# Attention, two products and a routed expert layer on one core: conversion, weight product and the next stage's first products moved to later slots

## The chip, the core and the metric

The kernel runs on one core of a Trainium2 chip. Five engines each run their own instruction stream in order: TensorE (PE, with its weight loads shown apart as PEld), VectorE (DVE), ScalarE (ACT), GpSimd (POOL) and SyncE (SP), which here issues almost all DMAs. The metric is the time of one execution in microseconds; lower is better.

## The reference, cut to what matters

```python
# attention, B=2, H=8, S=768, D=64: a query sees only keys of its own hash bucket (6 sign bits)
mask = q_bucket[:, :, :, None] == k_bucket[:, :, None, :]
scores = np.where(mask, scale * q @ k.T, -1e9)
attn = softmax(scores); x = (attn @ v) laid out as [1536, 512]
# second part
h = (x @ w1) * (x @ w2) @ w3           # d_ff = 1024
x = h @ w_out                          # [1536, 512]
# third part: each token goes to the one expert of 8 with the largest logit
logits = x @ w_gate + modality_bias[modality_id]
out[mask] = gate_w[mask] * (relu(x[mask] @ e_w1[e]) @ e_w2[e])
```

All of it is float32. A product is made of three products of rounded high and low parts (`TERMS`). `w3 @ w_out` is formed once in the kernel (the "weight product", called w34), so that the second part is `(a * b) @ w34`.

## The kernel before

The heads are taken in pairs: 8 pairs of 2 heads, 6 query tiles each. Everything up to the middle of the kernel is one loop over slots `i` from 0 to 109. A slot's work is written out by hand, and each engine keeps the written order:

- **First products and maxima** (`stage_1`, unit `i`, slots 0 to 95): PE forms a tile of scores `m` (2 matmuls), and DVE takes its row maximum (`TENSOR_REDUCE`, line 348). After 6 units (3 query tiles of 2 heads) four small operations (lines 352 to 355, result `nm`) prepare the maxima; they run on POOL. `stage_f` transposes them on PE (`f`), ACT copies them (`rT`), and two DMAs put them as two extra rows under `q`.
- **Second products** (`stage_2`, unit `j = i - 9`, slots 9 to 104): PE forms the scores `s` with the maximum already subtracted (4 matmuls), ACT takes the exponential into `pt` (line 377), and POOL adds `pt` into `acc`. `stage_a` multiplies `pt` with `v` two slots later (`a`, 4 matmuls). In slots 25 to 84 (`GROUP`) two of these are done together in every second slot. `z`, `n`, `wt`, `pg` are small products for hash bits, row sums and the gate's weights.
- **Conversion**: `w1`, `w2`, `w3`, `w_out` arrive as 64-bit numbers and are made float32 on DVE in 3 steps for each of 40 pieces (`L508`, `L509`, `L498`, issued by `fill`). A piece of `w3` or `w_out` is split into its high part on ACT and its low part on POOL (line 490); a piece of `w1` or `w2` goes out to DRAM (`wfd`). `RAMP` says how many pieces are wanted by which slot, and `piece_load` brings a piece in.
- **Weight product** (`w34_step`): 192 matmuls `w` in 8 rounds of 24, at `W34_STEP` for each slot and at most 7 at once, as soon as their pieces are converted. After a round ACT copies PSUM out (`ev`), and only then the next round can begin.
- **SWITCH** (slot 86): the 40 pieces and 192 matmuls are done, their memory is given back, and the 16 pieces of `w1` and `w2` come back from DRAM (`st`), are split on ACT and DVE (line 490), `RATE2` of them for each slot. From `SWITCH + NSTEP` the first chunk of tokens is split as well (`norm_step`).
- **The next stage's first products** (`moe_half`, `ab`, 12 matmuls): from slot `EARLY` = 95 one half for each slot, until `NEARLY` = 5 of the first chunk's 8 columns are done. The rest follows behind the loop, without the attention's work beside it.

Scores `m` and `s` share one PSUM tag with two buffers; which of the two a tile gets is settled when the program is built. So an `m` waits either for the reduction of the `m` before it (DVE), or, where the two have changed places, for the exponential of the `s` just ahead of it (ACT).

At the start PE fills gaps with products of the unit matrix (`busy`). SP's queue is in written order too: `load_pair` brings `q` and `k` of a pair (384 KB each), a piece is 512 KB.

The lines around the first slots:

```python
        if i == 4:
            load_pair(2)
        if i == 5:
            for m in range(3):
                piece_load(m)
        if i == 8:
            load_pair(3)
```

Of the kernel before, what the change touches and what calls it, by code (L numbers as in the profile page):

```python
# [8 lines left out]
F32 = mybir.dt.float32  # L9
# [4 lines left out]
ALU = mybir.AluOpType  # L14
# [11 lines left out]
C_MASK = float(2 ** 30)  # L26
# [6 lines left out]
NCH = NT // CH  # L33

PRE = 0
RAMP = ((7, 0), (19, 10), (84, 41))
RATE2 = 1.4
W34_STEP = 3.15
W34_MOST = 7
SWITCH = 86  # L40
LEAD = 9
NDVE = 0
ACC_DVE = ((76, ()), (96, (2,)))
# [2 lines left out]
RUN = 2  # L46
NP = 4
BUSY = {4: 2, 5: 4, 8: 2}
GROUP = (16, 76)
HASH = (4, 6)  # L50
PREL = 2
PREA = 2
# [2 lines left out]
HS = S // 2  # L55
KROWS = (78, 128)
NB = 12
EARLY = 95
ERATE = 1
NEARLY = 5  # L60
NSTEP = 4
PATTERN = (1, 1, 0, 1, 0)
HOOKS = (3, 24, 82)
RAWS = 4
# [34 lines left out]
def pieces_at(i):  # L99
    for (a, x), (b, y) in zip(RAMP, RAMP[1:]):  # L100
        if i < b:
# [62 lines left out]
def body(tc, qT, kT, vP, w1d, w2d, w3d, wod, mod, wgate, mbias, e1, e2, cst, out):  # L164
    nc = tc.nc
    PE, ACT, DVE, POOL, SP = nc.tensor, nc.scalar, nc.vector, nc.gpsimd, nc.sync
# [61 lines left out]
    NU = 2 * 6 * NPAIR  # L228
    raw_t, bt_t, head_t, v_t = {}, {}, {}, {}

    def load_pair(p):
        b, hp = divmod(p, HP)
        for nm, src in (("q", qT), ("k", kT)):
            t = r_raw([P, S])
            SP.dma_start(t, src[b, hp])
            raw_t[p, nm] = t
# [99 lines left out]
    def stage_1(u):  # L336
        p, qt, hd = u
        q, k = head_t[p, hd, "q"], head_t[p, hd, "k"]
        s = ps("s", [P, 2, 512], f"m{p}_{qt}_{hd}")
        for half in range(2):  # L340
            PE.matmul(  # L341
                s[:, half, 0:HS], q[0:KROWS[hd], 0, qt * P:qt * P + P], k[0:KROWS[hd], 0, half * HS:half * HS + HS],
                start=True, stop=True,
            )
        if qt % 3 == 0 and hd == 0:
            nm_t[p, qt // 3] = r_nm([P, 32])
        nm = nm_t[p, qt // 3]
        DVE.tensor_reduce(nm[:, 3 * hd + qt % 3:3 * hd + qt % 3 + 1], s[:, :, 0:HS], AX.XY, ALU.max, negate=True)  # L348
        if qt % 3 == 2 and hd == 1:
            v, fin = nm[:, 6:12], nm[:, 12:24].bitcast(F32R).rearrange("p (d x t) -> p d x t", d=2, x=2)  # L350
            v3 = v.rearrange("p (d t) -> p d t", d=2)
            POOL.tensor_scalar(v, nm[:, 0:6], C_MASK / 2, None, ALU.is_lt)
            POOL.tensor_mul(v, v, nm[:, 0:6])
            POOL.tensor_copy(fin[:, :, 0, :], v3)
            POOL.tensor_sub(fin[:, :, 1, :], v3, fin[:, :, 0, :].bitcast(F32))

    def stage_f(p, half):
        t = ps("m", [P, P], f"f{p}_{half}")
        PE.transpose(t[0:12, :], nm_t.pop((p, half))[:, 12:24], ident)
        rT = r_rT([12, P], F32R)  # L360
        ACT.copy(rT, t[0:12, :])  # L361
        for hd in range(2):
            r = brow(hd) + NB
            SP.dma_start(
                head_t[p, hd, "q"][r:r + 2, 0, half * HS:half * HS + HS].bitcast(F32),
                rT[6 * hd:6 * hd + 6, :].bitcast(F32),
            )
# [301 lines left out]
    def moe_half(ch, f, j, tag="ab"):  # L669
        x = x_t[ch]  # L670
        fs = slice(f * P, f * P + P)
        if j == 0:
            ab_t[ch, f] = ps(tag, [P, 2, CH], f"ab{ch}{f}")
        ab = ab_t[ch, f]
        for c in range(4):
            for i, (st, mv) in enumerate(TERMS):
                PE.matmul(ab[:, j, :], w12[j][:, st, c, fs], x[:, mv, c, :], start=(c == 0 and i == 0), stop=(c == 3 and i == 2))  # L677
        if j == 0:
            return
        if f % 4 == 0:  # L680
            gf_t[ch, f // 4] = rg["gf"]([P, 4, CH])
        gf = gf_t[ch, f // 4][:, f % 4, :]
        g = g_t[ch]
        asb = rg["asb"]([P, CH])
        ACT.copy(asb, ab[:, 0, :])  # L685
        DVE.tensor_mul(gf, asb, ab[:, 1, :])  # L686
        ACT.copy(g[:, 0, f, :], gf)  # L687
        POOL.tensor_sub(g[:, 1, f, :], gf, g[:, 0, f, :].bitcast(F32))  # L688
# [39 lines left out]
    for c in (102, 128):  # L728
        v = cs[:, c:c + 28].rearrange("p (j n) -> p j n", n=NB + 2)[:, :, 0:6]
# [47 lines left out]
    for i in range(NU + LEAD + NLAG + 1):  # L777
# [14 lines left out]
            rg["asb"] = ring("asb", CH, 1, True)  # L792
        if i == 0:
            load_v(0)
        if i == 4:
            load_pair(2)
        if i == 5:
            for m in range(3):
                piece_load(m)
        if i == 8:  # L800
            load_pair(3)
        if i == 12:
            SP.dma_start(cs[:, 160:], cst[:, 160:])
            SP.dma_start(wgs[:, :, 0:E], wgate.rearrange("(c p) e -> p c e", p=P))
        if 0 <= i - SWITCH - NSTEP < HP + 2:
# [18 lines left out]
        p, ph = divmod(i, 12)  # L824
# [3 lines left out]
        if i < NU:  # L828
            if p and ph == 9 and p + 3 < NPAIR:
                load_pair(p + 3)  # L830
            stage_1(units[i])
            fill()
            if long:
                fill()
        fi = i if i <= 6 else i - 1
        if fi % 6 == 0 and 0 < fi <= NU and (i <= 6 or fi > 6):
            stage_f(*divmod(fi // 6 - 1, 2))
        if p == 0 and ph in (1, 2):
            hash_z([1], ph - 1, "uw"[ph - 1])
# [34 lines left out]
            w34_step(quota - done["w"])  # L874
        for h in range(int((i - EARLY) * ERATE), int((i - EARLY + 1) * ERATE)):
            if 0 <= h < 2 * NEARLY:
                moe_half(0, h // 2, h % 2, "wm"[h // 2 % 2])
        if late and n % 12 == 4:
            late.pop(0)()
        if not both or len(dq) > 2:  # L880
# [298 lines left out]
    wu = {}  # L1179
# [360 lines left out]
```

## Time and profile before

| | |
|---|---|
| median of 3 runs | 686.21 us (685.7 to 687.42) |
| the profiled execution: its own time | 685.69 us |
| the profiled execution: span, first to last instruction | 683.9 us |
| PE busy | 651.8 us of the span (95%) |
| DVE, POOL, ACT busy | 386.3, 317.8, 314.0 us |
| granted clock of PE, mean | 0.998 of 2.4 GHz |

The span is 1.8 us shorter than the execution's own time. A row of the stretches gives start and end, length, each engine's busy time with its instructions in the order PE, PEld, DVE, ACT, POOL, then PE's granted clock (1.00 is 2.4 GHz), the DMA engines' busy share and GB/s. A row of the timeline gives an instruction's start, how long it took, the engine and line, what it writes and reads, how many were merged, and in brackets how long the engine sat idle just before and what released it. A matmul's time includes its way through the pipeline, so rows of PE overlap: what a group costs PE is read from one group's start to the next.

### The profile page before, as it was taken

The numbers are of one execution on the slowest core, as the hardware profiler recorded it, in microseconds if no ns is written. First come the engines' busy times: TensorE is split into PE (matmuls) and PEld (weight loads), VectorE is DVE, ScalarE is ACT, GpSimd is POOL, SyncE is SP. The second block draws the span as 40 slices with busy tenths as digits, with TensorE's granted clock in tenths as the row PEclk, the third lists the DMA queues.
The fourth block names the chain that finished last, engine by engine and source line by source line (L and its number), as shares of the span: only waits on it lengthen the run. The fifth ranks groups of instructions, "written<-read, shape, count | busy, mean of one in ns | idle before, by whom it ended". The sixth has DMA issues, their size and how long they took to land. (4 is left out here: it accounts for less than half of the span.)

```text
span 683.9 us, 11034 instructions
## 1 busy us (share of the span) xinstructions
PE 651.8 (95%) x4038; PEld 511.9 (75%) x4038; DVE 386.3 (56%) x617; ACT 314.0 (46%) x534; POOL 317.8 (46%) x312
## 2 busy tenths in 40 slices
PE   7888999999999997999999999999999999999995
PEld 2544566666566754678989898989888899899984
DVE  6897676767586889642632121121275865575550
ACT  7264665556556556553422121221224665564551
POOL 7498888687858776552524233231214212111110
PEclk9999999999999999999999999999999999999999
DMA  8755555473736463303201010100036977766630
GB/s 225 239 187 171 186 150 199 120 234 112 223 111 205 137 203 108 105 20 96 65 16 47 16 47 16 47 1 32 1 121 221 333 267 238 238 205 212 209 115 19
DMA packets 41691, 94.04 MB, mean 138 GB/s; under 512 B 6352, under 2 KB 12032, under 8 KB 41632
## 3 DMA queue, kind: packets, MB, share of 16 engines
q1 hardware_dynamic: 39552, 86.72, 40.7%
q0 software_dynamic: 2080, 6.56, 2.8%
q8 instruction: 34, 0.56, 0.4%
q14 instruction: 25, 0.20, 0.1%
HBM read 72.98 MB, written 12.94 MB: 126 GB/s over the span
## 5 line engine op out<-in xcount | busy, mean ns | idle before, releaser
L677 PE MATMUL ab<-x,w 128*128 128x256 f32 x1152 | 143.6, 284 | 1.3 <-ACT rT L361 0.7
L677 PEld LDWEIGHTS ab<-x,w 128*128 128x128 f32 x1152 | 140.6, 191 | 5.6 <-ACT asb L685 2.1
L383 POOL TENSOR_TENSOR acc<-acc,pt 128x770 f32<-128x770 f32 x61 | 113.5, 1861 | 23.8 <-ACT pt L377 21.3
L348 DVE TENSOR_REDUCE nm<-m 128x1 f32<-128x768 f32 x96 | 91.4, 955 | 56.7 <-PE m L341 56.5
L377 ACT ACTIVATE pt<-s 128x768 f32<-128x768 f32 x96 | 78.0, 813 | 89.3 <-PE s L376 86.2
L376 PEld LDWEIGHTS s<-q,k 128*128 128x128 f32 (+1 forms) x384 | 63.9, 189 | 43.8 <-issue 23.2
L376 PE MATMUL s<-q,k 128*128 128x384 f32 (+1 forms) x384 | 91.5, 360 | 2.8 <-ACT pt L377 2.1
L688 POOL TENSOR_TENSOR g<-gf,g 128x256 fp32r<-128x256 f32 x48 | 35.6, 741 | 123.1 <-ACT g L687 119.8
L1206 DVE TENSOR_TENSOR eu<-er,eu 128x1024 fp32r<-128x1024 f32 x56 | 68.0, 1232 | 23.4 <-ACT eu L1205 21.6
L391 PE MATMUL a<-pt,v 128*64 128x385 f32 x384 | 76.4, 504 | 0.0
L686 DVE TENSOR_TENSOR gf<-asb,ab 128x256 f32<-128x256 f32 x48 | 20.2, 421 | 97.0 <-ACT asb L685 96.9
L1369 PE MATMUL e1F<-ex,eu 128*128 128x256 f32 x576 | 70.3, 283 | 0.5 <-DVE ex L1335 0.3
L1369 PEld LDWEIGHTS e1F<-ex,eu 128*128 128x128 f32 x576 | 69.7, 190 | 1.4 <-DVE ex L1335 0.5
L1395 POOL DMA_INDIRECT out<-o,sidx x13 | 13.7, 1051 | 122.3 <-ACT o L1394 106.2
L1387 PE MATMUL e2F<-eu,h 128*128 128x512 f32 x288 | 68.8, 394 | 0.0
L341 PE MATMUL m<-k,q 78*128 78x384 f32 x192 | 52.0, 353 | 11.1 <-ACT pt L377 5.7
L1387 PEld LDWEIGHTS e2F<-eu,h 128*128 128x128 f32 x288 | 53.3, 188 | 11.1
L1205 ACT CAST eu<-er 128x1024 fp32r<-128x1024 f32 x56 | 57.6, 1046 | 8.1 <-DMA er<-e 7.8
L1002 PE MATMUL x2p<-w,g 128*128 128x512 f32 x240 | 58.1, 396 | 0.0
L591 PE MATMUL w<-wo,w 128*128 128x512 f32 x192 | 51.4, 400 | 2.2 <-ACT ev L594 1.6
L1002 PEld LDWEIGHTS x2p<-w,g 128*128 128x128 f32 x240 | 44.2, 188 | 11.4 <-issue 2.1
L685 ACT COPY asb<-ab 128x256 f32<-128x256 f32 x48 | 17.9, 373 | 73.7 <-PE ab L677 73.7
(203 smaller groups left out, 800.1 us busy)
## 6 DMA issues: line engine op xcount, KB each, us to landing
er<-e SPq DMA_DIRECT2D x56, 512.0 KB
cr<-w3d SPq DMA_DIRECT2D x16, 512.0 KB
cr<-wod SPq DMA_DIRECT2D x8, 512.0 KB
cr<-w1d SPq DMA_DIRECT2D x8, 512.0 KB
wfd<-cT SPq DMA_DIRECT2D x16, 256.0 KB
cr<-w2d SPq DMA_DIRECT2D x8, 512.0 KB
st<-wfd SPq DMA_DIRECT2D x16, 256.0 KB
raw<-kT SPq DMA_DIRECT2D x8, 384.0 KB
```

The source lines that it names most:

```text
L341: PE.matmul(s[:, half, 0:HS], q[0:KROWS[hd], 0, qt * P:qt * P + P], k[0:KROWS[hd], 0, half * HS:half * HS + HS], start=True, stop=True,)
L348: DVE.tensor_reduce(nm[:, 3 * hd + qt % 3:3 * hd + qt % 3 + 1], s[:, :, 0:HS], AX.XY, ALU.max, negate=True)
L376: PE.matmul(s[:, hd, 0:HS], k[0:n, i, c * P:c * P + P], q[0:n, i, cl], start=(i == 0), stop=(i == 1))
L377: ACT.activation(pts[j % NP][:, :, 0:HS], s[:, :, 0:HS], AF.Exp, scale=SCALE)
L383: (DVE if on_dve else POOL).tensor_add(acc, pts[(j - 1) % NP] if c == 1 else acc, pts[j % NP])
L391: PE.matmul(a_t[p, half][64 * hd:64 * hd + 64, :], v[:, c, 64 * hd:64 * hd + 64], pts[j % NP][:, hd, :], start=(c == 0), stop=(c == QT - 1 ...
L677: PE.matmul(ab[:, j, :], w12[j][:, st, c, fs], x[:, mv, c, :], start=(c == 0 and i == 0), stop=(c == 3 and i == 2))
L1002: PE.matmul(st["ps"], g_t[ch][:, a, f, i * P:i * P + P], w34[b][:, f, :], start=(f == 0 and k == 0), stop=(f == 7 and k == 2),)
L1205: ACT.copy(t[:, 0, sl], raw)
L1206: DVE.tensor_sub(t[:, 1, sl], raw, t[:, 0, sl].bitcast(F32))
L1369: PE.matmul(o[f], w[:, st, c, fs], x[:, mv, c, :], start=(c == 0 and i == 0), stop=(c == 3 and i == 2))
L1387: PE.matmul(o, h[:, st, f, sl], w[:, mv, f, :], start=(f == 0 and k == 0), stop=(f == 7 and k == 2))
```

## The change

Numbers that set the order are replaced, the four small operations on the first pair's maxima go from POOL to DVE, the first pair's first `stage_f` is written ahead of unit 6 and not behind it, and the loads of the third and fourth pair, of the first three pieces and of two small tables are written 1 to 3 slots later. `moe_half` takes its PSUM under tags `w` and `u` in turn (it was `w` and `m`).

```diff
-RAMP = ((7, 0), (19, 10), (84, 41))
-RATE2 = 1.4
-W34_STEP = 3.15
+RAMP = ((8, 0), (22, 8), (89, 41))
+RATE2 = 1.6
+W34_STEP = 3.25
-SWITCH = 86
+SWITCH = 92
-GROUP = (16, 76)
+GROUP = (18, 82)
-EARLY = 95
+EARLY = 101
-NEARLY = 5
-NSTEP = 4
+NEARLY = 4
+NSTEP = 2
...
-            POOL.tensor_scalar(v, nm[:, 0:6], C_MASK / 2, None, ALU.is_lt)
-            POOL.tensor_mul(v, v, nm[:, 0:6])
...
+            eng = DVE if p == 0 else POOL
+            eng.tensor_scalar(v, nm[:, 0:6], C_MASK / 2, None, ALU.is_lt)
+            eng.tensor_mul(v, v, nm[:, 0:6])
...
-        if i == 4:
+        if i == 7:
             load_pair(2)
-        if i == 5:
+        if i == 8:
             for m in range(3):
                 piece_load(m)
-        if i == 8:
+        if i == 11:
             load_pair(3)
-        if i == 12:
+        if i == 13:
...
+            if i == 6:
+                stage_f(0, 0)
             stage_1(units[i])
...
-        fi = i if i <= 6 else i - 1
-        if fi % 6 == 0 and 0 < fi <= NU and (i <= 6 or fi > 6):
+        fi = i - 1
+        if fi % 6 == 0 and 6 < fi <= NU:
             stage_f(*divmod(fi // 6 - 1, 2))
...
-                moe_half(0, h // 2, h % 2, "wm"[h // 2 % 2])
+                moe_half(0, h // 2, h % 2, "wu"[h // 2 % 2])
```

**DVE, slots 9 to 13.** Before, three conversion steps stand behind the reductions of slots 10 and 11, and so on in every slot to 14 (`u`, `cT` are a piece's steps; `m_5_0` is pair 0's tile 5, head 0):

```order
L348 TENSOR_REDUCE nm_226<-m_4_1_259 128x1
L348 TENSOR_REDUCE nm_226<-m_5_0_274 128x1
L508 TENSOR_SCALAR u_279<-cr_202 128x512
L509 SCALAR_TENSOR_TENSOR u_279<-cr_202,u_279 128x512
L498 SCALAR_TENSOR_TENSOR cT_278<-cr_202,u_294 128x512
L348 TENSOR_REDUCE nm_226<-m_5_1_295 128x1
```

Of the change, the same engine at the same place:

```order
L348 TENSOR_REDUCE nm_222<-m_4_1_255 128x1
L348 TENSOR_REDUCE nm_222<-m_5_0_270 128x1
L348 TENSOR_REDUCE nm_222<-m_5_1_286 128x1
L353 TENSOR_SCALAR nm_222<-nm_222 128x6
L354 TENSOR_TENSOR nm_222<-nm_222 128x6
L355 CAST nm_222<-nm_222 128x2x3
L356 TENSOR_TENSOR nm_222<-nm_222 128x2x3
L509 TENSOR_SCALAR u_295<-cr_235 128x512
L510 SCALAR_TENSOR_TENSOR u_295<-cr_235,u_295 128x512
L499 SCALAR_TENSOR_TENSOR cT_294<-cr_235,u_295 128x512
L348 TENSOR_REDUCE nm_316<-m_0_0_313 128x1
L348 TENSOR_REDUCE nm_316<-m_0_1_331 128x1
```

The first piece stands in slot 11, behind the four small operations, and slots 12 and 14 have no piece; up to slot 23 eight pieces are done in slots 11, 13, 15, 16, 18, 20, 22 and 23.

**SP, around the first maxima's transfers (`rT`).** Before:

```order
L235 DMA raw_187<-qT 128x768
L235 DMA raw_189<-kT 128x768
L305 DMA k_18_87<-k_18_87 64x768
L305 DMA k_19_88<-k_19_88 64x768
L463 DMA cr_202<-wod 128x512
L463 DMA cr_204<-wod 128x512
L463 DMA cr_206<-wod 128x512
L364 DMA q_12_81<-rT_230 2x3x128
L364 DMA q_13_82<-rT_230 2x3x128
L235 DMA raw_241<-qT 128x768
L235 DMA raw_243<-kT 128x768
L305 DMA k_18_87<-bt_234 14x768
```

Of the change:

```order
L305 DMA k_18_87<-k_18_87 64x768
L305 DMA k_19_88<-k_19_88 64x768
L365 DMA q_12_81<-rT_215 2x3x128
L365 DMA q_13_82<-rT_215 2x3x128
L235 DMA raw_227<-qT 128x768
L235 DMA raw_229<-kT 128x768
L464 DMA cr_235<-wod 128x512
L464 DMA cr_237<-wod 128x512
L464 DMA cr_239<-wod 128x512
L305 DMA k_18_87<-bt_224 14x768
L305 DMA k_19_88<-bt_224 14x768
L305 DMA q_16_85<-bt_224 14x768
```

The two loads of the third pair and the three pieces went from ahead of `rT` to behind it, and they now stand right ahead of the second pair's hash bits (`bt`).

**PE, slots 90 and 91, with what each instruction waits for.** Before:

```order
L376 MATMUL s_1_3_2499<-q_12_81,k_14_83 128x384 [waits Activation_49]
L376 MATMUL s_1_3_2499<-q_12_81,k_14_83 128x384
L376 MATMUL s_1_3_2499<-q_13_82,k_15_84 128x384 x2
L341 MATMUL m_3_1_2512<-k_19_88,q_17_86 128x384 [waits DMAHW4_49,Activation_49]
L341 MATMUL m_3_1_2512<-k_19_88,q_17_86 128x384
L359 MATMUL f_0_2516<-ident_70,nm_2350 12x128 [waits Pool_49]
L391 MATMUL a_1_2475<-pt_20_89,v_2040 64x385 x2
L376 MATMUL s_1_4_2524<-q_12_81,k_14_83 128x384 [waits DVE_49]
```

Of the change:

```order
L377 MATMUL s_1_3_2482<-q_12_81,k_14_83 128x384 [waits Activation_49]
L377 MATMUL s_1_3_2482<-q_12_81,k_14_83 128x384
L377 MATMUL s_1_3_2482<-q_13_82,k_15_84 128x384 x2
L341 MATMUL m_3_1_2489<-k_19_88,q_17_86 128x384 [waits DVE_49]
L341 MATMUL m_3_1_2489<-k_19_88,q_17_86 128x384
L360 MATMUL f_0_2495<-ident_70,nm_2301 12x128 [waits Activation_49,Pool_49]
L583 MATMUL pt_2501<-ident_70,wT_2426 128x128 [waits Activation_49]
L392 MATMUL a_1_2471<-pt_20_89,v_1970 64x385 x2
```

Before, `m` waits for ACT and the `s` behind it for DVE: the buffers have changed places there, and in slots 20 and 21 as well. In the change every `m` from slot 9 to the last waits for DVE and no place has them changed. Behind the last `m` (slot 95) the change has slots 96 to 100 with `s` and `a` alone, and four `ab` halves in slots 101 to 104, the other four behind them; before, `ab` stands in every slot from 95 to 104.

## Rows read from the trace of the kernel before

**Rows 1.** The page's first section: busy time of each engine.

```profile
PE   651.8 (95%) x4038; PEld 511.9 (75%) x4038; DVE 386.3 (56%) x617; ACT 314.0 (46%) x534; POOL 317.8 (46%) x312
```

**Rows 2.** Stretches between `s` of slots 9, 30, 82, 92, 95, 104: busy, clock, DMA.

```profile
24.09:86.32 62.23, 54.13 (x271) 30.35 (x269) 49.16 (x66) 34.34 (x51) 50.39 (x46) 1.00 0.58 179
86.32:241.38 155.06, 151.61 (x848) 103.49 (x844) 112.40 (x150) 89.11 (x137) 118.90 (x97) 1.00 0.54 164
241.38:266.87 25.49, 22.59 (x121) 12.59 (x119) 22.14 (x29) 14.77 (x25) 21.15 (x18) 1.00 0.58 170
266.87:276.65 9.78, 6.95 (x32) 3.44 (x30) 9.30 (x13) 5.56 (x10) 3.77 (x3) 1.00 0.45 149
276.65:306.66 30.01, 29.27 (x192) 21.65 (x190) 16.66 (x27) 15.38 (x28) 15.70 (x15) 1.00 0.17 53
306.66:684.00 377.34, 368.80 (x2520) 331.38 (x2518) 160.19 (x314) 141.58 (x267) 92.28 (x110) 1.00 0.36 116
```

**Rows 3.** Timeline of PE, slot 11.

```profile
28.20 0.97 PE L376 MATMUL s<-q,k 78*128 78x384 f32 x4
29.70 0.62 PE L341 MATMUL m<-k,q 78*128 78x384 f32 x2 [0.53 <-DVE nm L348]
...
31.05 0.97 PE L376 MATMUL s<-q,k 78*128 78x384 f32 x4
```

**Rows 4.** Timeline of DVE over the same slot.

```profile
28.70 0.95 DVE L348 TENSOR_REDUCE nm<-m 128x1 f32<-128x768 f32 x1
29.57 0.68 DVE L508 TENSOR_SCALAR u<-cr 128x512 int32<-128x512 int32 x1
...
31.62 0.95 DVE L348 TENSOR_REDUCE nm<-m 128x1 f32<-128x768 f32 x1
```

**Rows 5.** Timeline of PE, a slot with no conversion beside it.

```profile
252.03 0.98 PE L376 MATMUL s<-q,k 78*128 78x384 f32 x4
252.85 0.51 PE L341 MATMUL m<-k,q 128*128 128x384 f32 x2
...
254.09 0.97 PE L376 MATMUL s<-q,k 78*128 78x384 f32 x4
```

**Rows 6.** Timeline of PE, slot 92.

```profile
266.87 0.97 PE L376 MATMUL s<-q,k 78*128 78x384 f32 x4
268.81 0.61 PE L341 MATMUL m<-k,q 128*128 128x384 f32 x2 [0.96 <-ACT pt L377]
...
270.15 0.97 PE L376 MATMUL s<-q,k 78*128 78x384 f32 x4
```

**Rows 7.** Timeline of PE, a slot with the weight product.

```profile
93.12 1.79 PE L591 MATMUL w<-wo,w 128*128 128x512 f32 x7
94.74 0.86 PE L376 MATMUL s<-q,k 78*128 78x384 f32 x4
```

**Rows 8.** Timeline of PE, where a round of the weight product begins.

```profile
130.45 0.73 PE L591 MATMUL w<-wo,w 128*128 128x512 f32 x2 [0.74 <-ACT ev L594]
```

**Rows 9.** Timeline of PE, an early half of the next stage.

```profile
288.74 1.58 PE L677 MATMUL ab<-x,w 128*128 128x256 f32 x12
290.26 0.87 PE L391 MATMUL a<-pt,v 128*64 128x385 f32 x4
```

**Rows 10.** The tile `st`: instructions of DVE and ACT, ns minimum/median/maximum.

```profile
L489 ACT CAST w<-st x16: 602/612/622, 260.1 to 297.8; 128x512 fp32r<-128x512 f32 x16
L490 DVE TENSOR_TENSOR w<-st,w x16: 678/747/2094, 261.3 to 298.5; 128x512 fp32r<-128x512 f32 x16
```

**Rows 11.** Timeline of POOL and PE ahead of slot 9.

```profile
16.84 0.24 POOL L352 TENSOR_SCALAR nm<-nm 128x6 f32<-128x6 f32 x1 [1.54 <-DVE nm L348]
...
21.80 2.74 PE L331 MATMUL busy<-ident 128*128 128x384 f32 x8
```

**Rows 12.** Two stretches of the first 24 us.

```profile
10.00:19.50 9.50, 8.99 (x37) 4.83 (x36) 8.06 (x10) 6.36 (x9) 6.70 (x8) 1.00 0.93 239
19.50:24.00 4.50, 4.36 (x15) 2.82 (x16) 4.24 (x6) 0.00 (x0) 0.17 (x1) 1.00 1.02 401
```

More of the change, by code (lines that the diff above doesn't have):

```diff
@@ L351, in stage_1 @@
             v3 = v.rearrange("p (d t) -> p d t", d=2)
-            POOL.tensor_scalar(v, nm[:, 0:6], C_MASK / 2, None, ALU.is_lt)
-            POOL.tensor_mul(v, v, nm[:, 0:6])
-            POOL.tensor_copy(fin[:, :, 0, :], v3)
-            POOL.tensor_sub(fin[:, :, 1, :], v3, fin[:, :, 0, :].bitcast(F32))
+            eng = DVE if p == 0 else POOL
+            eng.tensor_scalar(v, nm[:, 0:6], C_MASK / 2, None, ALU.is_lt)
+            eng.tensor_mul(v, v, nm[:, 0:6])
+            eng.tensor_copy(fin[:, :, 0, :], v3)
+            eng.tensor_sub(fin[:, :, 1, :], v3, fin[:, :, 0, :].bitcast(F32))
     def stage_f(p, half):
```

## The prediction

> **What bounds the kernel now.** PE. The page's totals come first: PE is busy for 651.8 of 683.9 us, no other engine for more than 387 [rows 1]. Then the stretches: behind slot 104 PE is busy for 368.8 of 377.3 us, and nothing there is edited but what passes into it, so the time can only change ahead of it; of the 30 us up to slot 104 all but 0.7 are PE's too [rows 2]. What is left is the attention loop, and there a busy PE is not a full one, since the pipeline of each small group counts as busy. So the third view is the timeline, read from one start of `s` to the next: a slot. A slot with `s`, `m` and `a` and nothing in the way takes 2.06 us [rows 5]. Two kinds of slot take more without more work on PE:
>
> - With a conversion beside it a slot takes 2.85 [rows 3]: the next `m` needs the buffer of the `m` before, and that one's reduction stands on DVE behind three conversion steps. From reduction to reduction DVE needs 2.92 [rows 4], so DVE sets the pace.
> - In slot 92, where the two buffers have changed places, `m` waits 0.96 for the exponential of the `s` just ahead, and the slot takes 3.28 [rows 6]. The three slots 92 to 94 take 9.78 [rows 2].
>
> Work of PE from start to start: `s` 0.82 [rows 5], `a` 0.80 [rows 9] (`z` and `n`, as many matmuls of 384 columns, I take for the same), 7 `w` 1.62, so 0.23 each [rows 7], an `ab` half 1.52 [rows 9]. A slot with `s` and `m` alone cannot be shorter than 1.94, from `s` through its exponential [rows 6].
>
> **The change part by part.** The sum goes by stretches. PE's work is kept, so what one stretch loses another gets.
>
> *Ahead of slot 9.* An `nm` operation takes 0.24 on POOL [rows 11]; on DVE no row shows one. Between nothing (DVE waits for `m` just behind them) and 4 x 0.24 = 0.96 I take 0.3. Loads behind `rT` instead of ahead of it gain nothing here: `s` starts at 24.09 [rows 2], when the eight `busy` products that begin at 21.80 and last 2.74 have been issued [rows 11], so PE and not the transfer sets that start. **+0.3**.
>
> *Slots 9 to 29*, 62.2 us now [rows 2]. The change has no `w` here. PE's work: 17 slots of 2.05, four grouped ones (twice 1.94, and twice some 2.6 with eight `a`), and three `z` or `n` and three small `f`: 34.9 + 9.1 + 2.7 = 46.7. Then the conversions: eight, in slots 11, 13, 15, 16, 18, 20, 22 and 23, where before ten stood in slots 10 to 20 and the rest followed at once. I walked the slots: a reduction begins 0.57 behind its `m` or when DVE is free, takes 0.95, and each step 0.7 [rows 4]; the next `m` begins 0.82 behind `s` or when that reduction ends. An isolated conversion costs 0.3 to 0.85, since the empty slot behind it drains DVE; those of slots 15 to 23, with hash bits and a subtraction among them, 4.6 together. That is 5.8 in all, and 0.3 more for `nm`, now in slot 11 on DVE. (The same walk over the slots of before gives 62.4.) Sum 52.8. **-9.4**. Of this, 6.4 is 24 `w` at 0.23 and some 0.9 of their small products, which move on; 3.0 is waiting saved. Bounds: if all eight cost 2.92 - 2.06 = 0.86 and the crowded slots as much again, +1.5; if only the crowded ones cost anything, -1.5.
>
> *Slots 30 to 81*, 155.1, of which PE idles 3.5 [rows 2]. Five `w` come in: +1.2. Where a round ends early in a slot the next waits for ACT's copy, 0.74 [rows 8]; such ends come as often as before, give or take one. I leave the idle time as it is: 0, between -1 and +1.5. **+1.2**.
>
> *Slots 82 to 91*, 25.5. The other 19 `w` and the small products: 5.3 more work. Slots 90 and 91 lose their changed buffers, 1.2 each as in slot 92, and a slot without filler (1.94) gets 7 `w`, which fills some 0.8 of its wait: -3.2. **+2.1**, with DVE's last conversions beside it up to +1 more.
>
> *Slots 92 to 94*, 9.8 [rows 2]. Three slots of 2.06: **-3.6**. The splits of `st` that crowd DVE there begin in slot 95 now.
>
> *From slot 95*, 30.0 to slot 104 [rows 2]. The change leaves three halves in slots 101 to 103 (3 x 3.12 = 9.4) and puts six behind (6 x 1.52 = 9.1). Slots 95 to 100 have `s`, `a` and one `n`: 1.62 of PE a slot, too little to cover the `st` splits, nine of which fall here. Floor: 1.94 a slot, with `n` 12.4. DVE needs 0.68 to 2.09 for a piece [rows 10], say 1.1, and has the chunk's splitting and scaling beside it. There are three raw buffers, and a load is issued when the piece three earlier is done: a load of between 1.1 (256 KB at 239 GB/s [rows 12]) and 4 us, taken as 2.7, 0.6 on ACT [rows 10], 1.1 on DVE and some waiting make 4.8 for three pieces, so at 1.6 pieces a slot 2.6 for a slot. Ceiling: slots as slow as slot 92's 3.28, 18.7 with one light one. I take 16.0, near the buffers' pace. Together 9.4 + 9.1 + 16.0 = 34.5. **+4.5**, between +0.9 and +7.2. This is the price: `ab` was what hid the splits.
>
> Sum: 0.3 - 9.4 + 1.2 + 2.1 - 3.6 + 4.5 = -4.9. From the profiled execution's own 685.7 that is 680.8; the median of the three runs, 686.2, lies 0.5 above it and would give 681.3. I forecast **681.0**.
>
> **A rule that speaks against it.** In slots 95 to 100 PE idles for a third of the time, in many small gaps. The trace has such a stretch: in slots 92 to 94 PE was busy for 6.95 of 9.78 us, and the granted clock stayed at 1.00, the 2.4 GHz level [rows 2]. The Trainium skill, "TensorE: Matmul & The Clock Gate", section "A second HAM failure mode: psum-queue depth-cycling", says that small idle times between groups of products can send the clock back and forth between its two levels. The trace of before does not bear that out. As a mechanism here: at 1.2 GHz the 10.5 us of PE's work in slots 95 to 100 would take 21 instead of the 16 forecast, and a few us behind them more: +6, 687.0.
>
> **The rivals.** *Hidden splits*: the gap runs at its floor, 12.4, since DVE's slow splits fall where POOL is idle: 677.4. For it: half the splits took 0.75 or less [rows 10]. *Given back*: the gap keeps the pace of today's slow slots, 18.7, and DVE in slots 82 to 91 costs 1 more: +3.7, 684.7, no change that can be measured. For it: where the splits stood, in slots 92 to 94, DVE was busy for 9.30 of 9.78 us [rows 2]. *It doesn't take*: the waits of slots 9 to 29 pass from DVE to POOL, busy there for 50.4 of 62.2 us [rows 2] with only some conversions less, and with the gap given back 686 is left. *Slower, by the loads*: 2 x 384 + 3 x 512 KB, 2.36 MB, now stand right ahead of the second pair's hash bits, which unit 12 needs at about 29 us. They can be issued from about 20. At the 401 GB/s of 19.5 to 24 us they take 5.9 us and are through by 26; at the 239 of the stretch ahead of it 9.9, through by 30, 1 us late [rows 12]. The change turns slower where they take over 29 + 4.9 - 20 = 13.9 us, below 170 GB/s; at 150, 15.7 us, it ends at 688. Against it: the 239 was reached with on-chip moves among the loads.
>
> **How the numbers follow.** Forecast 0.58, hidden splits 0.16, given back 0.13, doesn't take 0.06, slower by the loads 0.04, clock 0.03. The likeliest one's own range is 679 to 683.5, by the bounds of slots 9 to 29 and of the gap. Hidden splits reaches to 677, given back to 685: the range 677.0 to 685.0 leaves out the last three cases and a little at either end. A measurement of this kernel tells 0.3%, 2.1 us, from no change. So faster, below 684.1, is the forecast, hidden splits and nearly half of given back: 0.80. Within 0.3%: 0.13. Slower: 0.07.
>
> **What the profile of the changed kernel would show.** `s` of slot 9 at 24 to 24.5, of slot 30 at 75.5 to 79; no `m` anywhere that waits for an exponential; slots 86 to 94 of 2.0 to 3.1; slots 95 to 100 of 2.0 to 3.2, with ACT or PE idle behind the splits; four halves in the last slots and four behind the attention at 1.5; the granted clock at 1.00. I am wrong if `m` of unit 12 waits over 2 us for a transfer, if slots 95 to 100 take over 19 us, or if POOL sets the pace of slots 20 to 30.

## The result, and the profile after

The changed kernel takes 696.54 us (median of 4 runs, 691.89 to 697.61) against 686.5 for the kernel before beside it: a ratio of 1.0128, 95% interval 1.0105 to 1.0151. By the medians it is slower by 10 us, by the ratio by 8.8 (7.2 to 10.4), where 5 less were forecast. The profiled execution took 697.28 us; its span is 695.4, 11.5 more than before.

The page's busy times and its line of PE's granted clock, which answer to [rows 1]:

```profile
PE   660.2 (95%) x4038; PEld 516.4 (74%) x4038; DVE 396.6 (57%) x625; ACT 314.1 (45%) x534; POOL 317.4 (46%) x304
...
PEclk9979999999999999989999999999999999999998
```

PE does the same 4038 pieces of work and is busy for 8.4 us more. That is the first sign of a slower clock; the second line, the clock granted in each of 40 slices of the span, has dips in the third and the eighteenth. The stretches between the same starts of `s` as in [rows 2], and then steps of 2 us around the two dips:

```profile
25.73:87.78 62.05, 53.07 (x236) 28.20 (x234) 45.68 (x59) 32.03 (x48) 46.85 (x39) 0.89 0.58 166
87.78:244.16 156.38, 153.41 (x850) 104.23 (x848) 116.21 (x153) 89.96 (x139) 122.09 (x100) 1.00 0.57 167
244.16:273.46 29.30, 27.03 (x153) 17.17 (x152) 26.02 (x35) 13.22 (x21) 19.34 (x18) 1.00 0.55 178
273.46:279.61 6.15, 6.15 (x32) 3.60 (x31) 3.21 (x5) 3.06 (x5) 3.75 (x3) 1.00 0.45 131
279.61:309.70 30.09, 23.20 (x120) 14.34 (x118) 22.35 (x30) 17.56 (x32) 15.03 (x12) 0.89 0.30 98
309.70:695.40 385.70, 378.17 (x2592) 339.96 (x2590) 164.65 (x322) 144.97 (x275) 95.50 (x113) 1.00 0.36 115
...
30.00:32.00 2.00, 0.81 (x4) 0.49 (x4) 1.86 (x5) 0.81 (x1) 1.71 (x2) 1.00 1.03 217
32.00:34.00 2.00, 1.68 (x6) 0.58 (x6) 2.00 (x2) 0.00 (x0) 1.62 (x1) 0.72 1.01 210
34.00:36.00 2.00, 1.96 (x6) 1.14 (x4) 1.93 (x4) 0.27 (x1) 0.00 (x0) 0.50 0.49 182
40.00:42.00 2.00, 2.00 (x7) 1.33 (x8) 1.09 (x2) 1.00 (x2) 0.04 (x1) 0.50 0.44 68
44.00:46.00 2.00, 2.00 (x11) 1.15 (x11) 1.59 (x3) 0.81 (x1) 1.96 (x2) 1.00 0.00 0
...
294.00:296.00 2.00, 0.00 (x0) 0.00 (x0) 0.75 (x2) 0.62 (x2) 0.00 (x0) 0.93 0.78 239
296.00:298.00 2.00, 0.95 (x4) 0.30 (x4) 1.03 (x2) 2.00 (x4) 0.22 (x1) 0.50 0.39 137
300.00:302.00 2.00, 2.00 (x11) 2.00 (x10) 1.23 (x3) 1.73 (x3) 0.00 (x0) 0.50 0.34 92
302.00:304.00 2.00, 2.00 (x11) 1.20 (x11) 1.69 (x4) 0.11 (x1) 0.00 (x0) 0.86 0.16 58
```

Against [rows 2] the first `s` starts 1.6 us later; slots 9 to 29 take 62.05 where 52.8 were forecast; slots 30 to 81 take 1.3 more (forecast 1.2) and slots 92 to 94 take 3.6 less (forecast 3.6); slots 82 to 91 take 3.8 more (forecast 2.1). From slot 95 on it is 8.4 more (forecast 4.5). In both bad stretches PE first stands idle (busy 0.81 of 2 us the first time, 0 of 2 us the second) and goes on at a granted clock of 0.50, the 1.2 GHz level, for 10 us the first time and 7 the second.

The timeline of all engines, at three places: ahead of slot 9, slots 11 and 12, and slots 98 to 101. SPq is SP's queue, where a row is the issue of a DMA. A slot is read from one start of `s` to the next, so the `m` in slot 11 is that of unit 12, which the loop writes in its turn 12, ahead of slot 12's `s`.

```profile
16.35 1.80 POOL L294 TENSOR_TENSOR lo<-raw,lo 128x768 fp32r<-128x768 f32 x1 [1.44 <-ACT lo L291]
16.67 1.51 DVE L353 TENSOR_SCALAR nm<-nm 128x6 f32<-128x6 f32 x1
18.21 0.17 DVE L354 TENSOR_TENSOR nm<-nm 128x6 f32<-128x6 f32 x1
...
18.93 0.27 PE L360 MATMUL f<-ident,nm 128*12 128x128 f32 x1 [0.71 <-DVE nm L356]
...
26.29 1.54 SPq L305 DMA_DIRECT2D q<-bt  x2
29.68 1.83 POOL L384 TENSOR_TENSOR acc<-pt,pt 128x770 f32<-128x770 f32 x1 [11.53 <-ACT pt L378]
30.14 1.40 DVE L353 TENSOR_SCALAR nm<-nm 128x6 f32<-128x6 f32 x1
32.33 0.59 PE L341 MATMUL m<-k,q 78*128 78x384 f32 x2 [1.52 <-DMA q<-bt]
32.85 1.54 PE L392 MATMUL a<-pt,v 128*64 128x385 f32 x4
34.32 1.65 PE L377 MATMUL s<-q,k 78*128 78x384 f32 x4
...
286.63 4.07 POOL L384 TENSOR_TENSOR acc<-acc,pt 128x770 f32<-128x770 f32 x2 [0.74 <-ACT pt L378]
286.96 2.04 DVE L636 TENSOR_TENSOR x<-xT,x 128x256 fp32r<-128x256 f32 x1
287.45 1.34 SPq L365 DMA_DIRECT2D q<-rT  x2
288.93 2.05 DVE L642 TENSOR_TENSOR xT<-xT,rb 128x256 f32<-128x256 f32 x1
289.79 0.94 PE L377 MATMUL s<-q,k 78*128 78x384 f32 x4 [1.72 <-DMA q<-rT]
291.50 0.41 DVE L636 TENSOR_TENSOR x<-xT,x 128x256 fp32r<-128x256 f32 x1
294.39 0.62 ACT L490 CAST w<-st 128x512 fp32r<-128x512 f32 x1 [2.82 <-DMA st<-wfd]
296.52 0.47 ACT L399 COPY xT<-a 128x385 f32<-128x385 f32 x1
297.05 1.55 PE L392 MATMUL a<-pt,v 128*64 128x385 f32 x4 [4.63 <-ACT xT L399]
298.53 1.65 PE L377 MATMUL s<-q,k 78*128 78x384 f32 x4
```

At the first place a small operation on DVE takes 1.51 us, and the next 0.17: the first ends with POOL's `lo`, at 18.15 to 18.18. PE waits for the last of the four, since `f` now stands ahead of unit 6. At the second, `m` of unit 12 waits for the hash bits `q<-bt`, whose transfers are issued at 26.29 behind the moved loads; behind the wait `s` and `a` take 1.65 and 1.54 instead of 0.97 and 0.87. At the third, `a` waits 4.63 us for ACT's copy of `xT`, which stands in ACT's order behind casts of `st` pieces that wait for their loads; ahead of that DVE's operations of 0.41 take 2.04 beside two additions on POOL. There `s` of slot 99 waits 1.72 for `rT` as well: ACT had it ready at 285.45, but SP issued it at 287.45, behind two loads of `st` that waited for DVE's splits.

### The profile page after: what moved, and what is told of

Its sections match the earlier page's. It is cut to its first block, busy times and chain, and to the rows that moved or that the text cites. A ratio compares the mean times of both kernels' runs of the same rounds, so it can differ in the third digit from the quotient of the medians.

```text
span 695.4 us, 11036 instructions
## 1 busy us (share of the span) xinstructions
PE 660.2 (95%) x4038; PEld 516.4 (74%) x4038; DVE 396.6 (57%) x625; ACT 314.1 (45%) x534; POOL 317.4 (46%) x304
## 5 line engine op out<-in xcount | busy, mean ns | idle before, releaser
L377 PEld LDWEIGHTS s<-q,k 128*128 128x128 f32 (+1 forms) x384 | 66.1, 194 | 49.3 <-issue 27.4
L377 PE MATMUL s<-q,k 128*128 128x384 f32 (+1 forms) x384 | 94.0, 368 | 6.5 <-DMA q<-rT 4.5
L392 PE MATMUL a<-pt,v 128*64 128x385 f32 x384 | 79.8, 524 | 4.6 <-ACT xT L399 4.6
L384 POOL TENSOR_TENSOR acc<-pt,pt 128x770 f32<-128x770 f32 x16 | 29.6, 1849 | 49.3 <-ACT pt L378 45.2
```

Of the source, the lines that this page charges most:

```text
L377: PE.matmul(s[:, hd, 0:HS], k[0:n, i, c * P:c * P + P], q[0:n, i, cl], start=(i == 0), stop=(i == 1))
L384: (DVE if on_dve else POOL).tensor_add(acc, pts[(j - 1) % NP] if c == 1 else acc, pts[j % NP])
L392: PE.matmul(a_t[p, half][64 * hd:64 * hd + 64, :], v[:, c, 64 * hd:64 * hd + 64], pts[j % NP][:, hd, :], start=(c == 0), stop=(c == QT - 1 ...
```

## Experiments

Each time is a median beside the kernel before on the same chip; in brackets the ratio to it with its 95% interval.

### The front edits apart from the numbers

**numbers_only** is the change with the front edits undone (loads, the `nm` operations on POOL, `stage_f` behind the maxima):

```diff
-        if i == 7:
+        if i == 4:
             load_pair(2)
-        if i == 8:
+        if i == 5:
             for m in range(3):
...
-            eng = DVE if p == 0 else POOL
+            eng = POOL
...
-            if i == 6:
-                stage_f(0, 0)
             stage_1(units[i])
...
```

> The changed numbers alone: the loads of the third and fourth pair and of the first pieces, the four small operations on the maxima and stage_f are as before. Theory 1 (the loads behind the first maxima's transfers delay the second pair's hash bits, unit 12's m waits 1.5 us and PE then runs at half its clock for 10 us): s of slot 9 at 24.1, no m that waits for a transfer in slot 11, granted clock 1.00 from 30 to 45 us, slots 11 to 13 at some 7 us instead of 13.1, and the whole at 688 to 689. Theory 2 (the faster slots run into the bits and maxima anyway, wherever the loads stand): m of unit 12 still waits over 1 us, the clock falls, and the whole stays at 693 or more. In both the waits in slots 26 and 100 stay.

688.00 us (1.0025, 1.0009 to 1.0040), as theory 1 said. So the front edits cost 8.5 us of the 10 by the medians, 7.1 of the 8.8 by the ratios, and the numbers by themselves still gain nothing. The first stretch of numbers_only, slots 9 to 29, as a row of the stretches:

```profile
24.18:77.34 53.16, 47.41 (x235) 25.48 (x234) 42.30 (x55) 32.23 (x48) 46.39 (x39) 1.00 0.54 162
```

53.16, with the clock at 1.00: near the 52.8 of the prediction's walk, once the front edits are gone. That this execution comes so near is luck in part: in three further kernels below with the same instructions up to there (gap_busy, rate_12, acc_dve) the stretch takes 55.2 to 55.6, with a longer wait of `s` in slot 27. Slots 11 to 13 take 6.88 here, 13.12 in the change.

**loads_back** undoes the loads alone; `nm` stays on DVE.

```diff
-        if i == 7:
+        if i == 4:
             load_pair(2)
...
-        if i == 11:
+        if i == 8:
             load_pair(3)
```

> The change with only the loads at their old slots (4, 5, 8 and 12); the small operations stay on DVE and stage_f stays ahead of unit 6. Theory 1 (the loads are what delays the hash bits): the wait of 1.5 us and the half clock in slots 11 to 13 are gone, s of slot 9 stays at 25.7, the whole is at 689.5 to 690.5. Theory 2 (the small operations on DVE delay the bits): the wait stays, 695 or more.

693.57 (1.0110, 1.0082 to 1.0139). Neither expectation held. `m` of slot 11 no longer waits for a transfer and `s` of slot 9 starts at 24.36, but a slot later PE stands still for longer. The timeline of loads_back there:

```profile
28.31 1.84 POOL L384 TENSOR_TENSOR acc<-pt,pt 128x770 f32<-128x770 f32 x1 [9.29 <-ACT pt L378]
28.77 1.42 DVE L353 TENSOR_SCALAR nm<-nm 128x6 f32<-128x6 f32 x1
30.43 1.84 POOL L384 TENSOR_TENSOR acc<-acc,pt 128x770 f32<-128x770 f32 x1 [0.27 <-ACT pt L378]
30.62 1.67 DVE L356 TENSOR_TENSOR nm<-nm 128x6 fp32r<-128x6 f32 x1
32.21 0.68 DVE L509 TENSOR_SCALAR u<-cr 128x512 int32<-128x512 int32 x1
...
34.26 0.95 DVE L348 TENSOR_REDUCE nm<-m 128x1 f32<-128x768 f32 x1
35.27 1.01 PE L341 MATMUL m<-k,q 128*128 128x384 f32 x2 [3.78 <-DVE nm L348]
```

Of the four small operations two end with POOL's addition that runs beside them (28.31 + 1.84 = 30.15 against 28.77 + 1.42 = 30.19; 32.27 against 32.29). The four take 3.5 us; the first piece's three steps follow, and only then the reduction for which `m` waits 3.78. `m` then runs at half the clock. The Trainium skill, "SBUF — State Buffer", section "SBUF: two separate sides", says that VectorE and GpSimd share a pair of ports as an exclusive lock, held for the whole instruction while the other blocks, where the VectorE operation has two inputs in SBUF or runs in a mode that uses both ports. The end of line 356, which has two such inputs, agrees with it; line 353 has one, and no run here shows its mode.

**nm_pool** undoes only the move of `nm`; the loads stay late.

```diff
-            eng = DVE if p == 0 else POOL
+            eng = POOL
```

> The change with only the four small operations on the first pair's maxima back on POOL; the loads stay behind the first maxima's transfers, stage_f stays ahead of unit 6. Theory 1 (two independent faults: the late loads delay the hash bits, the small operations on DVE wait for POOL, and each alone empties PE once for long enough that its clock falls): s of slot 9 at 24.2 to 24.6, m of unit 12 still waits 1 to 2 us for a transfer, the clock falls to 0.50 behind it, slots 11 to 13 at 11 to 13 us, the whole 693 to 695. Rival (the small operations alone make the damage, the loads none): no such wait, 688 to 689.

691.06 (1.0071, 1.0048 to 1.0094; single runs from 688 to 694.6). `m` of slot 11 waits 1.60, and in this profile the clock is at 0.50 for some 3.4 us, so that slots 11 to 13 take 9.61. (The profile puts that wait down to a conversion step on DVE that ends just before; in numbers_only, with the loads early, the same `m` does not wait.) The theory's kind is right, its size too large. With numbers_only and the change the four make a square: by the medians late loads add 3.1 us (688.0 to 691.1), `nm` on DVE 5.6 (688.0 to 693.6), both 8.5. So each fault does damage without the other. That they just add up is not shown: by the ratios the single prices are 3.2 and 5.8 and both together 7.1, each with an interval of some 2 us either way. `stage_f` is ahead of unit 6 in three of the four, and its own price was not measured; ahead of slot 9 it is small, since in loads_back, where the four operations of the first maxima take 0.17 each, `s` starts at 24.36, 0.3 later than before.

**front_only** puts the front edits, all of them, on the kernel before.

```diff
-        if i == 4:
+        if i == 7:
             load_pair(2)
...
+        eng = DVE if p == 0 else POOL
...
+            if i == 6:
+                stage_f(0, 0)
             stage_1(units[i])
```

> The kernel before with the change's front edits alone: the loads at slots 7, 8, 11 and 13, the first pair's small operations on DVE, stage_f ahead of unit 6; all numbers as before. Theory 1 (the front edits cost by themselves what numbers_only saved against the change, 8.5 us): s of slot 9 at 25.7, a stall of over 1.4 us in slot 11 or 12 with the clock at 0.50 behind it, the whole 693 to 696. Rival (DVE's pace in slots 10 to 23, with a conversion in every slot, hides much of it, and the clock does not fall): 688 to 690.

693.24 (1.0095, 1.0077 to 1.0113): 6.7 us slower without any of the numbers. In its profile one small operation took 1.76 us beside POOL, PE was busy for 0.60 of the 2 us from 18, the clock was at 0.52 from 22 to 24, and `s` of slot 9 began at 27.60.

### The price of the clock

**busy_11** is the change with filler ahead of unit 11's `m`, one `m` ahead of the one that waits for the bits.

```diff
+            if i == 11:
+                busy(6, "m")
             stage_1(units[i])
```

> The change with six more products of the unit matrix (some 2.0 us of PE's time) written in slot 11 ahead of m; the load order, and so the wait for the hash bits, stays. Theory 1 (PE's clock fell because PE stood idle there): the clock stays at 1.00, slot 11 takes 4.0 to 4.6, slots 12 and 13 some 4.7 together instead of 8.6, the whole 692 to 693. Rival (the clock falls there for another reason, for instance what came before the stall): the clock is 0.50 again, the whole 697 or more.

694.42 (1.0117, 1.0100 to 1.0134), slower than the 692 to 693 expected. The granted clock stays at 1.00 from 26 to 46 us, with the loads as late as in the change. The filler took 3.6 us, not 2.0 (28.66 to 32.23, from its start to that of `m`), which cost part of what the clock gave back. It also pushed unit 12's `m` to 34.57, when the bits had landed, so the wait itself was gone. That agrees with PE's idle time letting the clock fall, but the wait and the fall were not taken apart here; gap_busy below does that for slot 100.

**after_clock** is the change with such filler, in better sizes, near all three stalls (two products ahead of unit 11's `m`, four ahead of `s` in slot 27, six behind `s` of slot 100).

```diff
+            if i == 11:
+                busy(2, "m")
             stage_1(units[i])
...
+        if i == 101:
+            busy(6, "m")
         while (long or not both) and next_a[0] <= min(j - AGE, NU - 1):
...
+            if i == 27:
+                busy(4, "m")
             stage_2(j)
```

> The changed kernel whole, with products of the unit matrix in three stretches in which PE stood idle: two ahead of m in slot 11 (1.3 us), four ahead of s in slot 27 (2.7 us), six ahead of the a behind slot 100's s (4.0 us). The waits stay, only the idle time ahead of the falls of the clock is filled; the difference to the change is the price of the clock. Theory 1 (the clock fell because PE stood idle, and it cost about 0.7 + 3.4 us in slots 11 to 13, 1.3 in 27 and 28, 2 in 101): granted clock 1.00 throughout, 688.5 to 690.5. Rival (the waits themselves make up the loss): 694 or more.

690.48 (1.0066, 1.0043 to 1.0089): 6.1 us less than the change by the medians, 4.3 by the ratios. The clock stays at 1.00 in all three stretches, and the rival (694 or more) is out. But this is not the price of the clock alone. The profiled execution is the fastest of the four, and in it the waits have changed as well: `m` of unit 12 waits 0.56 instead of 1.52, `s` of slot 9 starts at 24.48 instead of 25.73, though nothing is edited ahead of it, and the fault of `nm` is absent, which is a matter of a few tenths of a microsecond:

```profile
16.69 0.17 DVE L353 TENSOR_SCALAR nm<-nm 128x6 f32<-128x6 f32 x1
17.30 1.85 POOL L294 TENSOR_TENSOR lo<-raw,lo 128x768 fp32r<-128x768 f32 x1 [1.45 <-ACT lo L291]
...
28.45 1.82 POOL L384 TENSOR_TENSOR acc<-pt,pt 128x770 f32<-128x770 f32 x1 [9.30 <-ACT pt L378]
30.19 0.17 DVE L353 TENSOR_SCALAR nm<-nm 128x6 f32<-128x6 f32 x1
30.80 0.17 DVE L356 TENSOR_TENSOR nm<-nm 128x6 fp32r<-128x6 f32 x1
31.85 1.85 POOL L384 TENSOR_TENSOR acc<-acc,pt 128x770 f32<-128x770 f32 x1 [1.59 <-ACT pt L378]
```

These are the same operations ahead of POOL's `lo` and in the gap between two of POOL's additions (the second L353 starts 0.08 before the first addition ends): 0.17 each. How much of the 6.1 is the clock's is open.

### The numbers, and the thin slots 95 to 100

**ramp_only** is the kernel before with three lines changed:

```diff
-RAMP = ((7, 0), (19, 10), (84, 41))
+RAMP = ((8, 0), (22, 8), (84, 41))
-W34_STEP = 3.15
+W34_STEP = 3.25
-GROUP = (16, 76)
+GROUP = (18, 82)
```

> The kernel before with RAMP ((8, 0), (22, 8), (84, 41)), W34_STEP 3.25 and GROUP (18, 82) alone: fewer conversions up to slot 22, the rest of the change undone. By the prediction's terms slots 9 to 29 fall from 62.2 to 52.5, of which some 7 us come back as weight products later: 683 to 684.5. Theory 1 with the maxima's transfers as the next bound (s of slot 27 waited 2.8 us for q in the changed kernel): slots 9 to 29 at 55 to 56, the whole at 686 to 688. Rival (fewer conversions gain nothing there): slots 9 to 29 at 58 or more, the whole at 689 or more.

688.21 (1.0020, 1.0006 to 1.0035). Slots 9 to 29 take 54.0, 8.2 less than before, between the 52.5 of the prediction's terms and the 55 to 56 of theory 1. Slots 30 to 81 give 3.3 back and slots 82 to 91 another 4.8. So all of the 8.2 is given back, where the prediction let 6.4 of its 9.4 come back as moved work and counted the other 3.0 as waiting saved; why the rest comes back too is not shown.

**gap_busy** adds to numbers_only five products ahead of the `a` behind slot 100's `s`.

```diff
+        if i == 101:
+            busy(5, "m")
         while (long or not both) and next_a[0] <= min(j - AGE, NU - 1):
```

> The kernel with the changed numbers alone (numbers_only) and five more products of the unit matrix, 3.3 us of PE's time, written ahead of the a behind slot 100's s, where PE stood idle for 4 us behind ACT. If the clock fell because of that idle stretch: the clock stays 1.00 there, slot 101 takes 3.1 to 3.4 instead of 5.06, the wait of slot 100 stays, 685.5 to 686.5 for the whole. Rival (the clock falls anyway, or the products cost what the clock gives): 687.5 or more.

685.30 (0.9983, 0.9973 to 0.9994). ACT's copy of `xT` still comes late, and slots 95 to 100 take 18.1 (18.8 in numbers_only), but with PE kept busy the clock stays at 1.00 and slots 101 to 103 take 9.36 instead of 11.33, the prediction's 9.4. Here 2 us were the clock's: the idle time let it fall, not the wait.

**rate_12** slows the splits in numbers_only.

```diff
-RATE2 = 1.6
+RATE2 = 1.2
```

> numbers_only with RATE2 1.2 instead of 1.6: the splits of the pieces that come back from DRAM are written later, so that fewer of ACT's casts stand ahead of its copy of xT while their loads are still under way. Theory 3 (ACT waits in its order for these loads, and a waits behind it): slots 95 to 100 at 15 to 16.5 instead of 18.8, slot 101 at 3.1 to 3.4 and the clock at 1.00, the whole 682.5 to 685. Rival (DVE, slowed beside POOL, sets the pace there, or the splits that now stand behind slot 104 hold up the halves): 687 or more.

686.85 (1.0002, 0.9986 to 1.0018), outside the range expected. Slots 95 to 100 shrink from 18.8 to 16.8, but `a` still waits 3.27, and slot 101 takes 5.19 at the half clock.

**acc_dve** takes POOL's additions out of the stretch:

```diff
-ACC_DVE = ((76, ()), (96, (2,)))
+ACC_DVE = ((76, ()), (86, (2,)), (96, (1, 2, 3, 4, 5)))
```

> numbers_only with all additions into acc from unit 86 (slot 95) on DVE instead of POOL, so that POOL has next to nothing in slots 95 to 100. If DVE's operations of 2.0 to 2.5 us there (0.4 to 0.7 elsewhere) wait for POOL's additions, and the raw buffers, the loads and ACT's casts are late because of them: DVE's splits at 0.7 each, slots 95 to 100 at 14 to 16.5 instead of 18.8, slot 101 at 3.1, the whole 683.5 to 685.5. Rival (three raw buffers and the loads set the pace by themselves): slots 95 to 100 at 18 or more, 687 or more.

684.93 (0.9971, 0.9950 to 0.9992). Slots 95 to 100 take 15.51. DVE has four more additions in these slots and its other operations are short again, as its timeline shows:

```profile
280.98 0.96 DVE L384 TENSOR_TENSOR acc<-acc,pt 128x770 f32<-128x770 f32 x1
281.85 1.29 DVE L491 TENSOR_TENSOR w<-st,w 128x512 fp32r<-128x512 f32 x2
283.05 0.42 DVE L636 TENSOR_TENSOR x<-xT,x 128x256 fp32r<-128x256 f32 x1
```

An addition takes 0.96 here (1.83 on POOL), and `x` 0.42 where it took 2.04. But ACT's loads still hold `a` for 2.56, and the clock still falls.

**rate_busy** joins RATE2 1.2 with filler in slots 27 and 100.

```diff
-RATE2 = 1.6
+RATE2 = 1.2
...
+        if i == 101:
+            busy(4, "m")
...
+            if i == 27:
+                busy(3, "m")
```

> A version that could beat both kernels: numbers_only with RATE2 1.2, three products of the unit matrix ahead of s in slot 27 and four ahead of the a behind slot 100's s. By the terms measured so far: slots 24 to 29 at 15.5 to 16.5, slots 95 to 100 at 16 to 17, slots 101 to 103 at 9.4, the clock at 1.00: 682.5 to 684.5. If the filler delays what waits behind it: 686 or more.

684.80 (0.9972, 0.9962 to 0.9982), just above the range expected.

**switch_90** moves the switch two slots ahead, so that halves stand in slots 99 and 100 (against numbers_only, with the filler of slot 27 as in rate_busy).

```diff
-RAMP = ((8, 0), (22, 8), (89, 41))
-RATE2 = 1.6
+RAMP = ((8, 0), (22, 8), (87, 41))
+RATE2 = 1.2
-SWITCH = 92
+SWITCH = 90
-EARLY = 101
+EARLY = 99
```

> numbers_only with the switch two slots earlier (RAMP's end 87, SWITCH 90, EARLY 99), RATE2 1.2 and the three products ahead of s in slot 27: slots 99 and 100 now have a half each, so that slots 95 to 98 alone are thin. By the terms measured: the stall of 4 us and the half clock go, slots 95 to 98 at 10 to 12, 99 to 103 at 3.1 to 3.5 each, one more slot with changed buffers (1 us): 682 to 685. Rival (the splits are not ready by slot 99 and the halves wait for them on PE): a wait of over 2 us ahead of ab in slot 99 or 100, 687 or more.

687.44 (1.0015, 0.9996 to 1.0034): no gain. The wait ahead of `ab` in slot 99 is 1.17, below the rival's 2, but slots 92 to 94 take 10.37 instead of 6.15, with `s` waiting 2.62 for `rT` and `m` 1.30 for DVE: the splits only press on two slots earlier.

**rate_acc** joins acc_dve with RATE2 1.2, two repairs that each took only a part, and puts three products ahead of `s` in slot 27 (against acc_dve):

```diff
-RATE2 = 1.6
+RATE2 = 1.2
...
+            if i == 27:
+                busy(3, "m")
             stage_2(j)
```

> acc_dve with RATE2 1.2 and three products of the unit matrix ahead of s in slot 27; nothing fills slot 100. acc_dve took POOL's additions away and slots 95 to 100 still took 15.5 us, with 2.6 us of ACT's loads in slot 100. If both causes add up (DVE beside POOL, and casts written ahead of their loads): slots 95 to 100 at 13 to 14.5, the wait in slot 100 under 1.5, slot 101 at 3.1 to 3.4 and the clock at 1.00, 682 to 684 for the whole. If the three raw buffers set a floor of their own: slots 95 to 100 at 15 to 16 with 2 us or more of wait in slot 100 and the clock at 0.50 behind it, 684 to 686.

680.92 (0.9914, 0.9899 to 0.9930), below the 682 to 684 expected and clearly faster than both kernels; gap_busy, acc_dve and rate_busy were faster than the kernel before by 0.3% at most. Its slots 95 to 100 and 101 to 103:

```profile
269.57:282.83 13.26, 11.40 (x60) 5.28 (x58) 12.40 (x22) 10.04 (x19) 3.71 (x5) 1.00 0.28 87
282.83:292.19 9.36, 9.36 (x63) 7.16 (x61) 6.99 (x12) 5.34 (x9) 0.74 (x1) 1.00 0.32 106
```

13.26 is near the floor of 12.4, the clock stays at 1.00, and the wait in slot 100 is 1.31. Slots 95 to 100 lost 2.0 us by RATE2 1.2 alone, 3.3 by the additions alone and 5.5 by both. So POOL beside DVE and the rate of the splits made up the stall together; the three raw buffers are no floor of their own at this rate. That the rate acts through ACT's casts ahead of their loads is argued: a lower rate also puts fewer splits into these slots, and that was not tried apart.

**rate_busy_acc** adds the filler of slot 100 to it.

```diff
+        if i == 101:
+            busy(4, "m")
         while (long or not both) and next_a[0] <= min(j - AGE, NU - 1):
```

> rate_acc with four products of the unit matrix (2.7 us) ahead of the a behind slot 100's s: every repair in one kernel. If a wait in slot 100 remains, the filler hides it and keeps the clock: 682 to 684. If rate_acc has removed the wait, the filler costs up to 2.7 us and this is slower than rate_acc.

682.89 (0.9935, 0.9922 to 0.9949): slower than rate_acc, as the second case said. In these runs filler paid where the wait was longer than itself (gap_busy: 3.4 us in a wait of 4.0) and cost where it was shorter (2.7 us in a wait of 1.3).

## Why the prediction was wrong, point by point

Against the profile of before, -4.9 was forecast and +11.5 measured in the change's profile. Of the 16.4 us between them 9.2 lie in slots 9 to 29, 3.9 from slot 95 on, 1.7 in slots 82 to 91 and 1.3 ahead of slot 9. Two of the signs of being wrong that the prediction named came close and stayed below their marks: `m` of unit 12 waited 1.52 us, not over 2, and slots 95 to 100 took 18.92, not over 19.

**Ahead of slot 9** (forecast +0.3, measured +1.6). The failed step is the price of `nm` on DVE, "between nothing and 4 x 0.24". The upper bound was no bound: it was taken from POOL's own duration, and left out what POOL does at that moment. The rows of the kernel before, which that step read for the duration alone, show no DVE operation of the kind; the change's show 0.17 when POOL is idle and 1.40 to 1.66 when an operation of POOL's began just before. Where POOL's `lo` begins later, the forecast holds: in the profiles of loads_back and after_clock `s` of slot 9 starts at 24.36 and 24.48, 0.3 and 0.4 later than before. The change and after_clock have the same instructions up to there, so which of the two engines begins first differs between executions.

**Slots 9 to 29** (forecast 52.8, measured 62.05). The walk over conversions and reductions came near: 53.16 in numbers_only, 55.2 to 55.6 in three kernels with the same instructions up to there, where `s` of slot 27 waits longer and the clock falls behind it. Two steps beside it failed, and they are most of what made the change slower. "Loads behind `rT` instead of ahead of it gain nothing" looked only at `s` of slot 9. The rival "slower, by the loads" had the mechanism and the place, and got its threshold wrong: it let the loads start at 20 and put the hash bits last at 29. In the change they were issued from 21.1, the bits behind them only at 26.29, and with the bits' own transfers among the loads the rate was 217 and 210 GB/s from 30 to 34; the bits had landed when `m` began at 32.33. The forecast let the change turn slower only below 170 GB/s, since it priced the lateness at its own length; a wait of 1.52 was enough, with the half clock behind it. The chance for it was 0.04. The 0.3 for `nm` in slot 11 failed as above: in loads_back it is a wait of 3.78.

**The clock** (rival at 0.03, for slots 95 to 100 only). It fell, to the level that the rival named, but not among many small gaps: it fell behind single stalls, ahead of `m` in slot 11, of `s` in slot 27 and of `a` in slot 100. The one in slot 27, in the change:

```profile
78.95 0.95 PE L377 MATMUL s<-q,k 78*128 78x384 f32 x4 [2.81 <-DMA q<-rT]
...
82.00:84.00 2.00, 2.00 (x7) 1.52 (x6) 0.57 (x1) 0.48 (x1) 1.56 (x2) 0.50 0.00 0
```

The section of the Trainium skill that the prediction weighed, on small idle times between groups, is not what this case shows (in rate_acc slots 95 to 100, with PE busy for 11.40 of 13.26 us, stay at 1.00); the same page, "TensorE: Matmul & The Clock Gate", section "HAM oscillation — how this bites in real kernels", describes waits for transfers behind which the next work starts at the lower clock, and the trace agrees: 0.50 behind the wait for `q<-bt`, though the waits of that section are longer than the 1.52 us here. The length of a stall did not decide by itself: behind a wait of 1.51 us (`s` of slot 27 in nm_pool) the clock stayed at 1.00. The prediction costed every stall at its own length; here a stall of 1.5 us drew 10 us at half the clock behind it.

**Slots 30 to 81 and 92 to 94** (+1.2 and -3.6 forecast, +1.3 and -3.6 measured). Right, by their own steps; no `m` waits for an exponential.

**Slots 82 to 91** (+2.1, up to +1 more; measured +3.8). The direction was right and the size too small. DVE's last conversions stand beside the first chunk's scaling there: slot 87 takes 4.82, with 0.56 of wait for a reduction and 0.69 for a small one on DVE.

**From slot 95** (+4.5, between +0.9 and +7.2; measured +8.4). In numbers_only it is +9.5, so this miss does not come from the front edits. The stretch behind slot 104, with six halves more, is 8.4 longer (forecast 9.1). Slots 95 to 100 took 18.92, just past the ceiling of 18.7; the step took 1.1 for a split on DVE out of the 0.68 to 2.09 of [rows 10] without asking which of those rows stood beside an addition on POOL, and had neither ACT's casts ahead of `xT` nor SP's loads ahead of `rT` among its waits. Slots 101 to 103 took 11.17 instead of 9.4, which is the clock's, as gap_busy shows. rate_acc shows that the forecast 16.0 was too long for that stretch without these two faults, and too short with them.

**What stays open.** Slots 24 to 29 have a wait of `s` in slot 27 for `rT` which differs between executions: four kernels with the same instructions up to there (numbers_only, gap_busy, rate_12, acc_dve) took 15.46, 17.67, 17.57 and 17.96, the first with the clock at 1.00. The waits were 1.22, 1.92, 1.86 and 2.27. What decides it was not tried apart from the filler, and neither was `stage_f` alone. How the change's loss divides between the waits and the clock behind them is open but for slots 101 to 103.

## What to carry to other kernels

An operation moved to an idle engine costs what the engines beside it make of it at that moment: read what runs on POOL in the same microsecond before pricing a DVE operation on on-chip memory. When loads are put behind a transfer, ask which small transfers stand behind the loads, and until when. A stall of PE is priced with the time at the lower clock that may follow it, up to 10 us here; where the stall can't be removed, products of matching length in it are cheap, and where it is short they cost more than they give.

## What the runs showed of the hardware that was not expected

- An operation on 128 x 6 elements took 0.17 us on DVE with POOL idle, and 1.40 to 1.76 with an operation on 128 x 768 or 770 that had begun on POOL just before, ending within 0.04 us of it in the cases shown. A subtraction on 128 x 256 went from 0.41 to 2.04.
- The additions into `acc` moved from POOL to DVE, an engine that was already the busier one there, made that stretch 3.3 us shorter (18.77 to 15.51).
- Behind a wait of 1.5 us, with PE busy for 0.81 of the 2 us around it, the granted clock was 0.50 from 33 to 43 us; with products ahead of it, which also removed the wait, it stayed at 1.00. In slot 100, where the wait for ACT stayed, products in it kept the clock at 1.00.
